# Moving the tasks of a software pipeline: attention and soft MoE on one core

## The chip, the cores and the metric

The kernel runs on one core of a Trainium2 chip. The metric is the device time of one execution in microseconds (us). A core has five engines with a queue each: TensorE (PE, matmuls, with its weight loads PEld), VectorE (DVE), ScalarE (ACT), GpSimd (POOL) and SyncE (SP), which here issues the DMAs. Each engine works through its own instructions in the order in which the program wrote them, and waits on semaphores for data and for free buffers.

## The reference

Eight batches of eight heads of attention with rotary positions, 576 positions of 64 elements each, all in float32. Its output, 4608 rows of 512, goes into a soft mixture of eight experts with four slots each.

```
q, k = rotate(q), rotate(k)
scores = (q @ k.T) / 8 - rowmax
x = (softmax(scores) @ v), heads side by side          # 4608 x 512
logits = x @ phi                                       # 4608 x 32
slot_input = softmax over the 4608 rows(logits).T @ x
slot_out[e] = relu(slot_input[e] @ w1[e]) @ w2[e]      # w1: 8 x 512 x 1024, w2: 8 x 1024 x 512
out = softmax over the 32 slots(logits) @ slot_out
```

## The kernel before

The 64 heads are worked on in 32 pairs; a pair fills the 128 partitions with two heads of 64. For pair p, called task(p), the steps are these.

`load0`, `load1` fetch the two halves of the tile `x_in` (q and k, each as the vector and its swapped copy, 576 KB a half; two buffers), and `load_v` fetches v, 576 KB. `spin0`, `spin1` multiply by cosine and sine on GpSimd, in four pieces each; `join`, the half addition, adds the two products on VectorE; `high0`, `high1` (ScalarE) and `low` (VectorE) split q and k into a high and a low float16 part (`hl`).

`m00` to `m31` and `m_rem` make rough scores from the high parts on TensorE, and VectorE reduces each to negated row maxima (L179, L187). `m_min` combines them, `m_turn` transposes them on TensorE, `m_half` (ScalarE) scales them to float16 (`mr`), and `m_rows` sends them by two small DMAs into the tile `peak` (L207, L208): these are the peak rows.

`t0` to `t8` make the transposed scores of 64 keys each, the first three products from `hl`, and the last product from `lift` and `peak`, which subtracts the maximum within the PSUM accumulation; ScalarE takes the exponential (L225). `av0` to `av8` multiply the weights by v (L240), `o_out` copies the result. `add1`, `add2` add weights of several blocks (L255, L258), `total` sums over the keys on TensorE (L268), `total_out` copies the sums, `send` spreads them over partitions by four small DMAs (`rc`, L279), `recip` inverts, `spread` writes them to DRAM (`r_row`, L292), `widen` reads them back as a broadcast to 64 partitions per head (`rb`, L299), and `norm` multiplies on GpSimd (L302). `logits`, `logits_sum`, `natural`, `natural_out` and, after every fourth pair, the statistics and slot work (`stats`, carried out piece by piece by `step0` to `step3`) follow. `weights` loads one 512 KB tile of expert weights per pair, `trickle0` to `trickle3` load more late in the run.

All tiles of scores, maxima, sums and transposes share one PSUM pool, `ps_s`, of three buffers (`bank2`); the weighted sums have one buffer of their own.

The order of the work is written out by hand. The dictionary `WHEN` gives every task a number; a beat handles one pair's share of all stages. The number modulo 4 is the task's place within the beat, its whole quotient by 4 the distance in pairs: a task with -12.8752 stands at 3.1248 of the beat and is done for the pair four ahead.

```
beat = sorted((when % 4, int(when // 4), name) for name, when in WHEN.items())
...
for p in range(NPAIR):
    for _, back, name in beat:
        do(name, p - back)
```

Since one loop emits all instructions, the sorted numbers set the order in each engine's queue, SyncE's DMAs among them. A prologue ahead of it does the first pairs' early steps, in the order of the unreduced numbers. After the loop the experts' two layers and the combination run with the loads of the remaining weights.

Of the kernel before, what the change touches and what calls it, by code (L numbers as in the profile page):

```python
# [44 lines left out]
RC = 12  # L45
PIECE = 4
WHEN = {
# [3 lines left out]
    "m_turn": -1.3908, "m_half": -1.1886, "m_rows": -0.6451, "weights": 0.144, "t0": 0.2257, "t1": 0.2781,  # L51
# [4 lines left out]
    "total_out": 5.5512, "send": 5.5526, "sums_turn": 6.0, "sums_wide": 6.3, "norm_wide": 6.4, "logits_late": 7.0,  # L56
    "recip": 7.022, "logits_sum_late": 7.05, "natural_late": 7.3, "natural_out_late": 7.35, "spread": 7.402,
    "widen": 7.6028, "norm": 9.5444, "logits": 10.5707, "logits_sum": 10.5777, "stats": 11.0576, "natural": 11.351,
    "natural_out": 11.3913,
}  # L60
QL, QH, KH, KL = range(4)
SUMS = ((0, 0, 0, True, False), (1, 0, 1, True, False), (2, 1, 0, True, False), (3, 1, 1, True, False),
# [873 lines left out]
```

## Time and profile before

| | before |
|---|---|
| time, median of 3 runs | 637.4 us (629.55 to 638.51) |
| the profiled execution | 634.23 us, span 632.4 us |
| TensorE busy | 547.5 us (87%) |
| VectorE busy | 447.0 us (71%) |
| ScalarE busy | 321.5 us (51%) |
| GpSimd busy | 283.5 us (45%) |
| SyncE's DMA queue | 110.15 MB, 52.7% of 16 engines' span |

Busy times come from one execution with a profiler; the span runs from its first instruction to its last. In a list of waits, "A <- B: total, times, longest" says how long engine A sat idle until B released it. In an answer by time, the columns are start, duration, engine, line, operation, output<-inputs, count, and in brackets the idle time before and what ended it; SPq is SyncE's issuing of a DMA, not the transfer. Rows that merge several instructions have the time from the first's start to the last's end.

### The profile page before, as it was taken

To read this page: it belongs to the slowest core of one execution; us is meant where nothing else is said; L and a number is where in the kernel's file an instruction comes from. 1 tells how busy PE (TensorE), PEld (TensorE's weight loads), DVE (VectorE), ACT (ScalarE), POOL (GpSimd) and SP (SyncE) were. 2 spreads that over 40 slices of the span, in tenths; PEclk is the share of its full clock that TensorE was granted. 3 is DMA by queue.
4 is the path that set the end of the run, shared out by engine and by line. 5 is a ranking of instruction groups with operands and counts; after the bars stand their busy time and mean duration, and the time that the engine had idled before them with its cause. 6 is when DMAs were issued, how large, how long until landed. Compare 5 with 4: busy or idle time off the path is not lost.

```text
span 632.4 us, 23700 instructions
## 1 busy us (share of the span) xinstructions
PE 547.5 (87%) x10320; PEld 368.5 (58%) x10320; DVE 447.0 (71%) x697; ACT 321.5 (51%) x647; POOL 283.5 (45%) x308
## 2 busy tenths in 40 slices
PE   3678979899988998898889998988899999799971
PEld 1356766666665666566666666666666666544550
DVE  6778757878877897688788988987889653222441
ACT  2145535566555555455555555655556554335341
POOL 2676654465456466544655655646556000100000
PEclk9679879999999999899999999999999999859995
DMA  7153434545554554455554545555542453549997
GB/s 263 46 188 115 142 120 168 168 168 169 169 167 167 168 169 168 167 168 163 174 168 166 170 165 170 169 167 170 167 135 98 128 194 126 177 142 345 348 373 258
DMA packets 71736, 111.66 MB, mean 177 GB/s; under 512 B 20176, under 2 KB 47568, under 8 KB 71632
## 3 DMA queue, kind: packets, MB, share of 16 engines
q1 hardware_dynamic: 71618, 110.15, 52.7%
q8 instruction: 81, 1.33, 0.9%
q14 instruction: 23, 0.19, 0.1%
q10 hardware_dynamic: 14, 0.00, 0.0%
HBM read 99.93 MB, written 9.58 MB: 173 GB/s over the span
## 4 chain that ended last, share of the span: by engine, by line
PE 54%; DMA 22%; DVE 11%; SPq 5%; ACT 3%; issue 2%; POOL 1%; ACTq 0%; POOLq 0%; DVEq 0%
PE s_ps L224 17%; DMA peak<-mr 14%; PE o_ps L240 11%; DVE nm L179 8%; PE s_ps L268 7%; PE s_ps L177 3%; PE s_ps L775 3%; DMA rb<-r_row 2%; SPq L279 2%; DMA r_row<-rr 2%; DMA x_in<-in_qk 2%; PE s_ps L351 1%; DMA w_exp<-in_w 1%; SPq L139 1%; ACT a_t L225 1%
## 5 line engine op out<-in xcount | busy, mean ns | idle before, releaser
L144 POOL TENSOR_TENSOR x_in<-x_in,cs_sb 128x288 f32<-128x288 f32 x248 | 231.6, 965 | 172.9 <-DMA x_in<-in_qk 163.1
L179 DVE TENSOR_REDUCE nm<-s_ps 128x2 f32<-128x576 f32 x256 | 186.2, 747 | 68.7 <-PE s_ps L177 68.0
L225 ACT ACTIVATE a_t<-s_ps 128x576 f32<-128x576 f32 x256 | 156.2, 648 | 90.7 <-PE s_ps L224 90.2
L240 PE MATMUL o_ps<-a_t,v_in 64*64 64x288 f32 x2048 | 168.6, 409 | 0.0
L224 PE MATMUL s_ps<-hl 64*64 64x288 f16 x3456 | 163.4, 289 | 5.3 <-DVE nm L179 2.6
L224 PEld LDWEIGHTS <-hl 64*64 64x64 f16 x3456 | 101.9, 107 | 45.0 <-issue 26.8
L224 PE MATMUL s_ps<-peak,lift 64*64 64x288 f16 x1152 | 98.9, 288 | 33.0 <-DMA peak<-mr 33.0
L177 PE MATMUL s_ps<-hl 64*64 64x288 f16 x1024 | 92.3, 295 | 11.5 <-DVE nm L179 7.6
L302 POOL TENSOR_TENSOR xt<-xt,rb 128x576 f32<-128x576 f32 x30 | 44.5, 1482 | 80.4 <-DMA rb<-r_row 48.8
L240 PEld LDWEIGHTS o_ps<-a_t,v_in 64*64 64x64 f32 x2048 | 75.2, 135 | 9.0 <-issue 0.2
L224 PEld LDWEIGHTS <-lift 64*64 64x64 f16 x1152 | 47.4, 108 | 40.5 <-issue 37.2
L273 ACT ACTIVATE s<-s_ps,bits 128x576 f32<-128x576 f32 x32 | 23.7, 740 | 85.2 <-PE s_ps L268 52.6
L177 PEld LDWEIGHTS <-hl 64*64 64x64 f16 x1024 | 47.9, 108 | 28.8 <-issue 21.1
L153 ACT CAST hl<-x_in 128x576 f16<-128x576 f32 (+1 forms) x66 | 40.6, 668 | 27.1 <-DVE x_in L148 25.3
L148 DVE TENSOR_TENSOR x_in<-x_in 128x1152 f32<-128x1152 f32 (+2 forms) x36 | 54.1, 1501 | 0.2
L255 DVE TENSOR_TENSOR c_t<-a_t 128x1152 f32<-128x1152 f32 x32 | 49.7, 1554 | 0.0
L157 DVE TENSOR_TENSOR hl<-x_in,hl 128x1152 f16<-128x1152 f32 x32 | 43.3, 1352 | 1.8 <-ACT hl L153 1.8
L268 PE MATMUL s_ps<-a_t,pick 128*32 128x288 f32 x384 | 36.7, 406 | 0.0
L343 ACT COPY xn<-s_ps 128x512 f32<-128x512 f32 x31 | 18.1, 585 | 19.3 <-PE s_ps L338 19.3
L248 ACT COPY xt<-o_ps 128x576 f32<-128x576 f32 x32 | 20.4, 638 | 12.1 <-PE s_ps L177 10.5
L240 PE MATMUL o_ps<-a_rem,v_in 64*64 64x288 f32 x256 | 25.8, 429 | 0.0
L187 DVE TENSOR_REDUCE nm<-s_ps 128x2 f32<-128x576 f32 x32 | 24.2, 758 | 0.8 <-PE s_ps L185 0.7
(182 smaller groups left out, 570.9 us busy)
## 6 DMA issues: line engine op xcount, KB each, us to landing
x_in<-in_qk SPq DMA_DIRECT2D x62, 576.0 KB
w_exp<-in_w SPq DMA_DIRECT2D x63, 512.0 KB
v_in<-in_v SPq DMA_DIRECT2D x32, 576.0 KB
rb<-r_row SPq DMA_DIRECT2D x60, 144.0 KB
out<-w_exp SPq DMA_DIRECT2D x16, 512.0 KB
rc<-s SPq DMA_DIRECT2D x120, 4.5 KB
x_in<-in_qk SPq DMA_DIRECT2D x4, 288.0 KB
out<-w_exp SPq DMA_DIRECT2D x4, 256.0 KB
```

What stands on the lines that cost most here:

```text
L144: eng.tensor_tensor(out=x[:, :, c], in0=x[:, :, c], in1=cs_sb[:, :, c], op=ALU.mult)
L148: nc.vector.tensor_tensor(out=x[:, t, 0, c], in0=x[:, t, 0, c], in1=x[:, t, 1, c], op=ALU.add)
L153: nc.scalar.copy(out=halves[p][:, 1 + t, c], in_=loaded[p][:, t, 0, c])
L157: nc.vector.tensor_tensor(out=hl[:, 0:4:3], in0=x[:, :, 0], in1=hl[:, 1:3], op=ALU.subtract)
L177: nc.tensor.matmul(s[rows[c], h, 0:HC], lhsT=hl[rows[h], QH, at:at + D], rhs=hl[rows[h], KH, half[n]], start=True, stop=True)
L179: nc.vector.tensor_reduce(out=nms[p][:, n, j:8:4], in_=s[:, :, 0:HC], axis=AX.X, op=ALU.max, negate=True)
L224: nc.tensor.matmul(s[rows[h ^ n], n, 0:HC], lhsT=lhs, rhs=rhs, start=(i == 0), stop=(i == 3))
L225: nc.scalar.activation(out=weights_of(p, b).rearrange("p (n x) -> p n x", n=2), in_=s[:, :, 0:HC], func=AF.Exp, scale=SCALE)
L240: nc.tensor.matmul(o[rows[h], n, 0:HC], lhsT=vt[r, b, n], rhs=a[r, half[n]], start=(b == 0), stop=(b == KB - 1))
L255: nc.vector.tensor_tensor(out=cts[p], in0=ats[p, 0], in1=ats[p, 1], op=ALU.add)
L268: nc.tensor.matmul(s[32 * i:32 * i + 32, n, 0:HC], lhsT=pick[:, n:n + NS], rhs=parts[cut][:, half[n]], start=first, stop=last, tile_positi ...
L302: eng.tensor_tensor(out=xts[p], in0=xts[p], in1=rbs.pop(p), op=ALU.mult)
```

## The change

Only the numbers in `WHEN` change. Which task does what, the buffers and the number of instructions are the same.

```diff
 WHEN = {
-    "load0": -16.0394, "load1": -12.8752, "spin0": -12.5438, "spin1": -11.4414, "join": -10.1083, "high0": -9.9771,
-    "high1": -9.8619, "low": -8.1718, "m01": -6.5475, "m00": -6.4604, "m10": -5.9309, "m11": -4.775, "m30": -3.8413,
-    "m20": -3.4941, "m21": -3.3162, "m31": -2.704, "m_rem": -2.4607, "m_min": -2.4496, "load_v": -2.2365,
-    "m_turn": -1.3908, "m_half": -1.1886, "m_rows": -0.6451, "weights": 0.144, "t0": 0.2257, "t1": 0.2781,
...
-    "t6": 3.0107, "av3": 3.0866, "av4": 3.222, "t7": 3.2246, "av5": 3.3, "t8": 3.4636, "trickle3": 3.55,
...
+    "load0": -16.2417, "load1": -12.7505, "spin0": -12.4293, "spin1": -12.3499, "join": -10.0149, "high0": -9.1292,
+    "high1": -9.0398, "low": -8.2534, "m01": -7.7418, "m11": -6.537, "m10": -5.8043, "m00": -5.1521, "m20": -3.9275,
+    "m21": -3.6837, "m30": -3.1916, "load_v": -2.9774, "m_rem": -2.8225, "m31": -2.6694, "m_min": -1.8172,
+    "m_turn": -1.7661, "m_half": -1.4738, "m_rows": -1.4517, "t0": -0.3716, "weights": 0.144, "t1": 0.1908,
...
+    "t6": 3.0107, "av4": 3.0368, "step2": 3.2977, "t7": 3.3041, "t8": 3.3085, "av5": 3.3336, "step3": 3.3449,
...
 }
```

Sorted by their places within a beat (the pair's distance from p in brackets), the tasks that put something on SyncE's queue and on the engines around the peak rows stand so:

```
SyncE before:   weights, trickle0, trickle1, send(-1), load_v(+1), trickle2, load1(+4), m_rows(+1),
                spread(-1), trickle3, widen(-1), load0(+5)
SyncE after:    weights, trickle0, load_v(+1), trickle1, send(-1), m_rows(+1), trickle2, load1(+4),
                spread(-1), widen(-1), trickle3, load0(+5)
TensorE before: av6(-1), m30(+1), t0, t1, av7(-1), m20(+1), av8(-1), m21(+1), t2, t3, m31(+1), av0, m01(+2),
                av1, m_rem(+1), m00(+2), total(-1), t4, t5, m10(+2), av2, logits(-2), m_turn(+1),
                t6, av3, av4, t7, m11(+2), av5, natural(-2), t8
TensorE after:  m20(+1), t1, av7(-1), m01(+2), av8(-1), m21(+1), t2, m30(+1), av0, m_rem(+1), t3, m31(+1), av1,
                m11(+2), total(-1), t4, t5, m10(+2), av2, av3, m_turn(+1), logits(-2), m00(+2),
                t6, av4, natural(-2), t7, t8, av5, av6, t0(+1)
VectorE before: m30, add2(-1), m20, m21, m31, m01, m_rem, m00, m_min(+1), join(+3), m10, logits_sum(-2), add1,
                recip(-1), m11, low(+3)
VectorE after:  m20, m01, m21, m30, m_rem, m31, m11, join(+3), m_min(+1), m10, logits_sum(-2), m00, add1,
                recip(-1), add2, low(+3)
GpSimd before:  spin1(+3), norm(-2), spin0(+4)
GpSimd after:   norm(-2), spin0(+4), spin1(+4)
```

An m unit stands in TensorE's list for its matmuls and in VectorE's for its reduction. The steps of the statistics are left out here: `step1` and `step2` stood together behind m10 before, and stand ahead of `total` and ahead of t7 after; `step0` follows av8 in both, `step3` follows t8 before and av5 after.

More of the change, by code (lines that the diff above doesn't have):

```diff
@@ L47 @@
 WHEN = {
[3 rows of a table removed]
-    "m_turn": -1.3908, "m_half": -1.1886, "m_rows": -0.6451, "weights": 0.144, "t0": 0.2257, "t1": 0.2781,
[4 rows of a table removed]
[L56 to L59, printed above, removed]
[3 rows of a table added]
+    "m_turn": -1.7661, "m_half": -1.4738, "m_rows": -1.4517, "t0": -0.3716, "weights": 0.144, "t1": 0.1908,
[4 rows of a table added]
+    "total_out": 5.55, "sums_turn": 6.0, "send": 6.1819, "sums_wide": 6.3, "norm_wide": 6.4, "logits_late": 7.0,
+    "logits_sum_late": 7.05, "recip": 7.2439, "natural_late": 7.3, "natural_out_late": 7.35, "spread": 7.3661,
+    "widen": 7.4052, "norm": 9.55, "logits": 10.7005, "logits_sum": 10.7559, "natural": 11.0423,
+    "natural_out": 11.2438, "stats": 11.3074,
 }
```

6 rows, old and new, of the table WHEN are left out of this document.

## Prediction

> **What bounds the kernel now.** I read the page's span and chain first, then the list of waits, then the DMA issues, the matmuls, VectorE and GpSimd of one repeated pair in the order of time.
>
> ```profile
> span 632.4 us, 23700 instructions
> ...
> PE s_ps L224 17%; DMA peak<-mr 14%; PE o_ps L240 11%; DVE nm L179 8%; PE s_ps L268 7%; PE s_ps L177 3%; PE s_ps L775 3%; DMA rb<-r_row 2%; SPq L279 2%; DMA r_row<-rr 2%; DMA x_in<-in_qk 2%; PE s_ps L351 1%; DMA w_exp<-in_w 1%; SPq L139 1%; ACT a_t L225 1%
> ```
> ```profile
> PE s_ps L224 <- DMA peak<-mr: 33.0, 22, 3.4
> ```
>
> The profiled execution took 634.23 us, of which 632.4 are the span. The chain that ended last is TensorE work, and the largest thing in it that is no work is the tiny DMA that puts the row maxima (the peak rows) into the tile `peak`: 14%. TensorE itself sat idle for it for 33.0 us in 22 waits.
>
> The steady part is one beat per pair of heads. I count beats by the four small DMAs of `send` (L279):
>
> ```profile
> 55.46 2.71 SPq L279 DMA_DIRECT2D rc<-s  x4
> ...
> 518.20 2.73 SPq L279 DMA_DIRECT2D rc<-s  x4
> ```
> ```profile
> 55.46:518.20 462.74, 421.30 (x8747) 294.69 (x8739) 369.38 (x557) 262.69 (x528) 244.06 (x250) 0.99 0.49 162
> ```
>
> From pair 0 to pair 29 that is 462.74 us for 29 beats: 15.96 us a beat. The second row is the table by stages (columns: length, busy time and count of PE, PEld, DVE, ACT, POOL, then granted clock, DMA share, GB/s). VectorE is busy 369.38 / 29 = 12.74 us of a beat, GpSimd 8.4; the granted clock is 0.99 and the DMA share 0.49, so neither is the limit as an average.
>
> One beat, by SyncE's queue:
>
> ```profile
> 299.59 2.74 SPq L279 DMA_DIRECT2D rc<-s  x4
> ...
> 315.27 2.73 SPq L279 DMA_DIRECT2D rc<-s  x4
> 318.10 0.39 SPq L163 DMA_DIRECT2D v_in<-in_v  x1
> 318.54 0.43 SPq L139 DMA_DIRECT2D x_in<-in_qk  x1
> 319.07 0.54 SPq L207 DMA_DIRECT2D peak<-mr  x1
> 319.65 0.54 SPq L208 DMA_DIRECT2D peak<-mr  x1
> 320.30 0.34 SPq L292 DMA_DIRECT2D r_row<-rr  x1
> 324.38 1.13 SPq L299 DMA_DIRECT2D rb<-r_row  x2
> ```
>
> `send` ends at 318.00. Before the peak rows (319.07) stand two large loads, v and the second half of x, 576 KB each. The same beat on TensorE, first the row of the chain for `total` (L268), then the matmuls in the order of time:
>
> ```profile
> 312.72 1.66 PE s_ps L268 x24
> ```
> ```profile
> 316.03 0.43 PE L351 MATMUL s_ps<-xt,phi_sb 128*32 128x128 f32 x8
> ...
> 316.50 0.28 PE L198 MATMUL s_ps<-id_sb,nm 128*9 128x128 f32 x1
> 316.70 0.56 PE L224 MATMUL s_ps<-hl 64*64 64x288 f16 x12
> ...
> 317.22 1.14 PE L240 MATMUL o_ps<-a_t,v_in 64*64 64x288 f32 x16
> 318.19 0.54 PE L224 MATMUL s_ps<-hl 64*64 64x288 f16 x12
> ...
> 318.80 0.66 PE L240 MATMUL o_ps<-a_t,v_in 64*64 64x288 f32 x8
> 319.39 0.66 PE L337 MATMUL s_ps<-id_sb,xt 128*128 128x128 f32 x4
> ...
> 320.08 0.56 PE L224 MATMUL s_ps<-hl 64*64 64x288 f16 x12
> ...
> 321.20 0.54 PE L224 MATMUL s_ps<-hl 64*64 64x288 f16 x12
> 323.60 0.54 PE L224 MATMUL s_ps<-peak,lift 64*64 64x288 f16 x4 [1.85 <-DMA peak<-mr]
> ```
>
> Durations overlap here, so I take the distance between starts as what a unit costs: scores t6 0.52, two weighted sums (av) 0.97, t7 with one m unit 0.61 (so t 0.50, m 0.11), `natural` 0.69, `logits` 0.47, `m_turn` 0.20. Let T be the start of `total`, 312.72. In t0 (321.20) the first twelve matmuls take three quarters of 0.50, so the peak rows are due at T+8.85; they come at T+10.88, 4.53 us after their first issue. **That is the wait, about 2 us in a beat, 33.0 in all.**
>
> **The change part by part.** No instruction is added or removed; tasks get other places. I sorted both tables by their fractional part to get each engine's order.
>
> *SyncE.* Before: send, v, x half 1, peak rows, r_row, broadcast rb, x half 0, weights. After: send, peak rows, x half 1, r_row, rb, x half 0, weights, v. The peak rows then issue when `send` ends, T+5.28, the second of them T+5.9, if `mr` is ready. From issue to landing without a large load ahead I have the row of `rc`: the last quarter of `send` begins at 317.32 and VectorE has its data at 319.55 (below), 2.2 us. So they land at T+8.1. The bounds: 2.2 us from the second issue, or, if the loads ahead were not the reason, 4.53 from the first (T+9.8). I take 2.2, the row of the same size class.
>
> *TensorE.* After `total` come t4, t5, m10, av2, av3, `m_turn`, `logits`, m00, t6, av4, `natural`, t7, t8, av5, av6, t0. Summed: 1.66 + 1.00 + 0.11 + 0.97 = T+3.74 for `m_turn` (before T+3.78), +0.20 +0.47 +0.11 +0.52 +0.49 +0.69 +1.00 +0.97 = T+8.19 for t0, so the peak rows are due at T+8.56. They land 0.4 earlier: the wait goes. The cover is thin: 0.4 us of lateness anywhere between `total` and the peak issue shows again as a wait on TensorE.
>
> *VectorE.* It runs in order and holds the half addition (`join`, L148), the evacuations and the additions:
>
> ```profile
> 311.25 1.42 DVE L179 TENSOR_REDUCE nm<-s_ps 128x2 f32<-128x576 f32 x2 [0.42 <-PE s_ps L177]
> ...
> 314.00 1.35 DVE L148 TENSOR_TENSOR x_in<-x_in 128x1152 f32<-128x1152 f32 x1
> ...
> 316.63 0.36 DVE L363 TENSOR_TENSOR l_sb<-s_ps,l_sb 128x192 f32<-128x192 f32 x1 [0.21 <-PE s_ps L354]
> 316.91 1.83 DVE L255 TENSOR_TENSOR c_t<-a_t 128x1152 f32<-128x1152 f32 x1
> 319.55 0.23 DVE L285 TENSOR_REDUCE rr<-rc 96x12 f32<-96x48 f32 x1 [0.81 <-DMA rc<-s]
> ...
> 321.06 1.35 DVE L157 TENSOR_TENSOR hl<-x_in,hl 128x1152 f16<-128x1152 f32 x1
> ...
> 323.00 0.75 DVE L258 TENSOR_TENSOR c_t<-c_t,a_t 128x576 f32<-128x576 f32 x1
> ```
>
> Two m evacuations come every 1.42 us. At T two of them are still queued in either order, so `join` starts near T+1.28 again (314.00). But `m_min`, which `m_turn` needs, now stands behind `join` instead of ahead: it is done at T+2.8 to T+3.3, for a `join` of 1.35 to 1.83 (the length to which the like addition L255 is drawn out), and due at T+3.74. Hidden, with 0.4 to 0.9 to spare.
>
> What is late next is VectorE itself. Its own work is 12.74 us a beat, and it must wait once: after m10 it stands at about T+3.7, and `logits` is done at T+4.41 plus the hand-over (0.2 in the row of L363), 0.9 us of idleness that no order of its own removes. That makes 13.6 us, the floor of the new beat. Today VectorE's larger idleness lies behind the peak wait. The floor assumes that nothing else collides; the first scores t0 now come ahead of m20 instead of behind m30, and seven m units in a row want VectorE between t0 and `total`, with only three score banks in PSUM.
>
> *Sum.* Two ways. Taking the wait alone: 33.0 / 29 = 1.14 a beat leaves 14.8. From the floor: half way between 13.6 and 15.96 is 14.8 too, half of the possible gain going to late beats (every fourth pair adds the statistics and slot work) and collisions. I take 14.8: 29 x 1.16 = 33.6 us less, 634.23 - 33.6 = **601 us**. The prologue issues t0 of pair 0 a little earlier, the tail from 540 us on is the same code: zero, with 5 us either way.
>
> *GpSimd and the shared data path.* Its order does not change (norm, spin0, spin1), but its inputs move:
>
> ```profile
> 312.14 1.41 POOL L302 TENSOR_TENSOR xt<-xt,rb 128x576 f32<-128x576 f32 x1 [1.34 <-DMA rb<-r_row]
> 314.62 4.78 POOL L144 TENSOR_TENSOR x_in<-x_in,cs_sb 128x288 f32<-128x288 f32 x4 [1.07 <-DMA x_in<-in_qk]
> 323.65 3.05 POOL L144 TENSOR_TENSOR x_in<-x_in,cs_sb 128x288 f32<-128x288 f32 x4 [4.25 <-DMA x_in<-in_qk]
> ```
>
> Four rotations take 3.05 us, or 4.78 when `join` and the c_t addition of VectorE run beside them. In the new order the norm (r_row issued T+7.7, landing behind x half 1 near T+11, rb 4 us later) runs near T+15 to T+16.4, just where the next `join` is due (T+14.8+1.28). The Trainium skill (SBUF — State Buffer, Who interferes with whom) says that a VectorE instruction with two SBUF inputs and a GpSimd instruction that reads SBUF exclude each other for the whole instruction; by that rule, which the stretched 4.78 agrees with, `join` could be held up to one norm, 1.41 us, and by it alone the beat would be up to 15.9, rival B's end.
>
> **The rivals.**
>
> *A: the early issue does not shorten the flight.* If 4.53 us stays, the rows land at T+9.8, and 1.25 of the 2.0 us remain: 0.75 x 22 = 17 us gained, **617**. Against it: the rows of v and x directly ahead, and 2.2 us for rc.
>
> *B: `join` becomes late.* x half 1 now issues behind the peak rows, T+6.5. Before, it took 318.54 to 323.65 = 5.1 us to arrive behind v; at 4 to 5 it is there at T+10.5 to T+11.5, rotated by T+13.6 to T+16.3, and `join` is due at T+16.1. If it or the norm holds `join` by a micro-second, `m_min`, `m_turn` and the peak rows slip with it, and the beat returns to 15.4 to 15.9: **618 to 634, middle 626**.
>
> *C: slower, by the broadcast.* x half 1 stands between the peak rows and r_row, so a large load is still ahead of r_row, rb and the norm, on which `logits` waits on TensorE. The chain of waits shows what that costs in a bad beat today:
>
> ```profile
> 207.81 4.46 DMA r_row<-rr
> ...
> 212.87 4.58 DMA rb<-r_row
> ...
> 217.60 2.54 POOL xt L302
> ```
>
> From 207.81 to 220.14 that is 12.3 us. With `recip` done at T+7.7, the norm ends at T+20.0, and `logits`, due at T+beat+3.94, makes the beat at least 16.1; with the 0.6 us by which step beats delay `recip`, 16.6: 29 x 0.65 = 19 more, **653**. It decides as soon as the three pieces exceed 10.9 us at a beat of 14.8. For it: the order in the queue. Against it: typical pieces are shorter (320.30 to 324.38 for r_row with twice the bytes ahead).
>
> *D: everything interleaves.* The beat comes to 13.6 to 14.2: 566 to 583, **575**.
>
> **How the numbers follow.** The forecast with its own range 588 to 616 gets 0.43, A 0.15, B 0.18, C 0.12, D 0.12. The range 582 to 636 takes in the forecast, A, B and the upper edge of D. 2%, about what a measurement can tell from no change, is 621.5 from the profiled time. Faster: the forecast, D and most of A, 0.67; within 2%: B and the rest, 0.21; slower: C, 0.12. The median of the runs shown, 637.4 (629.55 to 638.51), is 0.5% above the execution that I sum against.
>
> **What would show it.** Right: the wait of L224 for `peak` falls from 33.0 to under 8 us; the distance of `send` issues is near 14.8; peak rows issue directly behind `send` and land within 3 us; VectorE's busy share of the beat rises from 80% to 86%. Wrong: for A, 4 us between the peak issue and t0's last four matmuls; for B, VectorE idle ahead of L148, waiting for GpSimd; for C, TensorE idle ahead of L351, waiting for the norm; for D, no idleness of VectorE but ahead of L363. What would break the forecast most easily is the 0.4 us of slack between landing and t0.

## The result and the profile after

The changed kernel takes 595.5 us (median of 4 runs, 591.76 to 599.64) against 633.9 us (4 runs) of the kernel before: a ratio of 0.940, 95% interval 0.929 to 0.950. The profiled execution took 599.64 us, against 634.23 before. The forecast was 601, in a range of 582 to 636. Some executions show a lower granted clock and a longer time; the medians hold all runs, the ratios and their intervals leave those out, so a ratio need not be the quotient of the times beside it.

The page of the changed kernel, its span and its chain:

```profile
span 597.9 us, 23724 instructions
...
PE o_ps L240 14%; PE s_ps L224 14%; DMA rc<-s 7%; PE s_ps L268 6%; DVE nm L179 4%; PE s_ps L177 4%; DVE hl L157 3%; SPq L279 3%; PE s_ps L775 3%; DMA x_in<-in_qk 2%; DVE x_in L148 2%; DMA out<-w_exp 2%; PE s_ps L337 2%; DVE c_t L258 1%; DMA r_row<-rr 1%
```

The peak rows, 14% of the chain before, are no longer among the lines that the page lists for the chain. The waits, first of the changed kernel, then the two of before that the prediction did not show:

```profile
DVE nm L179 <- PE s_ps L177: 21.9, 28, 3.7
DVE l_sb L363 <- PE s_ps L354: 17.9, 22, 2.2
...
DVE l_sb L361 <- PE s_ps L354: 9.3, 8, 3.1
...
PE s_ps L224 <- DMA peak<-mr: 0.6, 3, 0.2
```
```profile
DVE nm L179 <- PE s_ps L177: 68.0, 84, 4.8
...
DVE l_sb L363 <- PE s_ps L354: 4.5, 12, 1.6
```

TensorE's wait for the peak rows went from 33.0 to 0.6 us. VectorE's wait for rough scores went from 68.0 to 21.9, and part of that idleness turned up ahead of `logits_sum` (L363, L361). The steady part, from the `send` of pair 0 to that of pair 29, in the table by stages:

```profile
57.25:486.95 429.70, 415.45 (x8763) 280.40 (x8755) 366.71 (x558) 264.64 (x528) 238.97 (x251) 1.00 0.54 173
```

429.70 / 29 = 14.82 us a beat, where the prediction had 14.8. The span divides so: ahead of the first `send` 57.25 (before 55.46, +1.8), the 29 beats 33.0 less, behind them 110.95 (before 114.20, -3.3): together 34.5 us less.

The same table tells where the 33.0 us of the beats come from. TensorE was idle for 41.4 of the 29 beats' 462.7 us before (462.74 - 421.30) and is idle for 14.3 of 429.7 now: 27.2 us less idleness, and 5.9 us less of its own work, though the matmuls are the same. Part of that last term can be seen in the granted clock. In the kernel before it falls to about half at three of the waits for the peak rows, those that end at 63.65, 82.54 and 258.55. Here is the second:

```profile
78.63 0.54 PE L224 MATMUL s_ps<-hl 64*64 64x288 f16 x12
82.54 0.63 PE L224 MATMUL s_ps<-peak,lift 64*64 64x288 f16 x4 [3.37 <-DMA peak<-mr]
82.73 1.15 PE L224 MATMUL s_ps<-hl 64*64 64x288 f16 x12
```

A group of twelve score matmuls takes 0.54 us ahead of that wait and 1.15 behind it; the mean granted clock is 0.57 from 64 to 68, 0.57 from 81 to 89 and 0.66 from 258 to 263, and these stretches lie in the three longest beats (17.24, 19.91 and 18.39 us). The changed kernel has one such stretch in its 29 beats, 267.9 to 272.0 with 0.58, behind a wait of 1.87 us at `m_turn`; e1 below has none. An estimate from these clocks and lengths: 6.9 us lost to them before, 1.7 after.

One beat of the changed kernel, SyncE, then TensorE's `total`, `m_turn` and t0, then VectorE and GpSimd of the next beat:

```profile
280.61 2.73 SPq L279 DMA_DIRECT2D rc<-s  x4
283.45 0.53 SPq L207 DMA_DIRECT2D peak<-mr  x1
284.03 0.53 SPq L208 DMA_DIRECT2D peak<-mr  x1
284.60 0.40 SPq L139 DMA_DIRECT2D x_in<-in_qk  x1
285.38 0.33 SPq L292 DMA_DIRECT2D r_row<-rr  x1
288.81 1.83 SPq L299 DMA_DIRECT2D rb<-r_row  x2
290.76 0.50 SPq L139 DMA_DIRECT2D x_in<-in_qk  x1
291.31 0.44 SPq L485 DMA_DIRECT2D w_exp<-in_w  x1
291.85 0.41 SPq L163 DMA_DIRECT2D v_in<-in_v  x1
294.35 3.82 SPq L279 DMA_DIRECT2D rc<-s  x4
...
298.86 0.53 SPq L208 DMA_DIRECT2D peak<-mr  x1
```
```profile
278.06 0.69 PE L268 MATMUL s_ps<-c_t,pick 128*32 128x288 f32 x8
...
281.85 0.28 PE L198 MATMUL s_ps<-id_sb,nm 128*9 128x128 f32 x1
...
286.42 0.54 PE L224 MATMUL s_ps<-hl 64*64 64x288 f16 x12
286.79 0.29 PE L224 MATMUL s_ps<-peak,lift 64*64 64x288 f16 x4
```
```profile
292.60 1.35 DVE L148 TENSOR_TENSOR x_in<-x_in 128x1152 f32<-128x1152 f32 x1
293.86 0.17 DVE L191 TENSOR_REDUCE nm<-nm 128x9 f32<-128x18 f32 x1
...
296.40 0.36 DVE L363 TENSOR_TENSOR l_sb<-s_ps,l_sb 128x192 f32<-128x192 f32 x1 [0.90 <-PE s_ps L354]
```
```profile
293.23 1.99 POOL L302 TENSOR_TENSOR xt<-xt,rb 128x576 f32<-128x576 f32 x1 [1.56 <-DMA rb<-r_row]
```

Here `total` starts at T = 278.06. The peak rows issue directly behind `send`, and t0's last four matmuls follow its first twelve without a gap.

### The profile page after: what moved, and what is told of

The parts are those of the page before. It is cut to its first block, busy times and chain, and to the rows that moved or that the text cites. A ratio compares the mean times of both kernels' runs of the same rounds, so it can differ in the third digit from the quotient of the medians.

```text
span 597.9 us, 23724 instructions
## 1 busy us (share of the span) xinstructions
PE 540.1 (90%) x10320; PEld 354.7 (59%) x10320; DVE 444.0 (74%) x697; ACT 323.5 (54%) x647; POOL 276.3 (46%) x308
## 4 chain that ended last, share of the span: by engine, by line
PE 56%; DVE 16%; DMA 15%; ACT 4%; SPq 4%; issue 3%; POOL 1%; DVEq 0%; ACTq 0%
PE o_ps L240 14%; PE s_ps L224 14%; DMA rc<-s 7%; PE s_ps L268 6%; DVE nm L179 4%; PE s_ps L177 4%; DVE hl L157 3%; SPq L279 3%; PE s_ps L775 3%; DMA x_in<-in_qk 2%; DVE x_in L148 2%; DMA out<-w_exp 2%; PE s_ps L337 2%; DVE c_t L258 1%; DMA r_row<-rr 1%
## 5 line engine op out<-in xcount | busy, mean ns | idle before, releaser
L144 POOL TENSOR_TENSOR x_in<-x_in,cs_sb 128x288 f32<-128x288 f32 x248 | 222.1, 928 | 148.5 <-DMA x_in<-in_qk 129.5
L179 DVE TENSOR_REDUCE nm<-s_ps 128x2 f32<-128x576 f32 x256 | 183.0, 750 | 22.8 <-PE s_ps L177 21.9
L225 ACT ACTIVATE a_t<-s_ps 128x576 f32<-128x576 f32 x256 | 160.3, 647 | 69.5 <-PE s_ps L224 64.2
L240 PE MATMUL o_ps<-a_t,v_in 64*64 64x288 f32 x2048 | 163.6, 408 | 1.1 <-ACT xt L248 0.3
L224 PE MATMUL s_ps<-hl 64*64 64x288 f16 x3456 | 159.6, 287 | 1.3 <-DVE nm L179 1.2
L224 PEld LDWEIGHTS <-hl 64*64 64x64 f16 x3456 | 100.1, 107 | 37.3 <-issue 25.8
L177 PE MATMUL s_ps<-hl 64*64 64x288 f16 x1024 | 83.8, 298 | 15.1 <-DVE nm L179 10.3
L224 PE MATMUL s_ps<-peak,lift 64*64 64x288 f16 x1152 | 90.5, 285 | 0.6 <-DMA peak<-mr 0.6
L177 PEld LDWEIGHTS <-hl 64*64 64x64 f16 x1024 | 44.0, 107 | 38.2 <-issue 21.7
L148 DVE TENSOR_TENSOR x_in<-x_in 128x1152 f32<-128x1152 f32 (+2 forms) x36 | 47.9, 1330 | 2.3 <-POOL x_in L144 2.0
L224 PEld LDWEIGHTS <-lift 64*64 64x64 f16 x1152 | 38.6, 108 | 3.0 <-issue 1.8
L248 ACT COPY xt<-o_ps 128x576 f32<-128x576 f32 x32 | 20.4, 638 | 16.0 <-PE o_ps L240 15.5
L187 DVE TENSOR_REDUCE nm<-s_ps 128x2 f32<-128x576 f32 x32 | 24.2, 755 | 2.1 <-PE s_ps L185 1.3
L258 DVE TENSOR_TENSOR c_t<-c_t,a_t 128x576 f32<-128x576 f32 x32 | 25.2, 788 | 0.1
```

The lines of the kernel that those rows point to most:

```text
L144: eng.tensor_tensor(out=x[:, :, c], in0=x[:, :, c], in1=cs_sb[:, :, c], op=ALU.mult)
L148: nc.vector.tensor_tensor(out=x[:, t, 0, c], in0=x[:, t, 0, c], in1=x[:, t, 1, c], op=ALU.add)
L177: nc.tensor.matmul(s[rows[c], h, 0:HC], lhsT=hl[rows[h], QH, at:at + D], rhs=hl[rows[h], KH, half[n]], start=True, stop=True)
L179: nc.vector.tensor_reduce(out=nms[p][:, n, j:8:4], in_=s[:, :, 0:HC], axis=AX.X, op=ALU.max, negate=True)
L224: nc.tensor.matmul(s[rows[h ^ n], n, 0:HC], lhsT=lhs, rhs=rhs, start=(i == 0), stop=(i == 3))
L225: nc.scalar.activation(out=weights_of(p, b).rearrange("p (n x) -> p n x", n=2), in_=s[:, :, 0:HC], func=AF.Exp, scale=SCALE)
```

## The experiments

The theory (Q): the gain is the queue, the large loads no longer directly ahead of the peak rows. The main rival (O): the gain is the new order of matmuls and reductions. Each ratio is against the kernel before on the same chip. The edits are to `WHEN` unless shown otherwise.

### The loads alone: e1_loads_only

The two entries alone, cut out of their lines:

```diff
 (on the kernel before)
-"load_v": -2.2365   "load1": -12.8752
+"load_v": -2.9774   "load1": -12.64
```

> The order of before, with only two loads moved on SyncE's queue: v to the place it has after the change, and the second half of x directly behind the peak rows. Theory Q (the gain is the queue: no large load ahead of the peak rows) expects the wait of L224 for peak to fall from 33.0 us to under 8, a beat near 14.9 and about 600 to 606 us. Rival O (the gain is the order of the matmuls and reductions, which needs t0, m_turn and the m units in their new places) expects at most half of the gain, 615 us or more, with VectorE idle for L177 staying near 68 us.

597.0 us (591.38 to 603.28), ratio 0.934 (0.927 to 0.942); a beat of 14.74 us.

```profile
DVE nm L179 <- PE s_ps L177: 30.4, 63, 3.1
DVE rr L285 <- DMA rc<-s: 15.5, 16, 2.2
PEld s_ps L351 <- POOL xt L302: 11.0, 8, 1.8
...
PE s_ps L351 <- POOL xt L302: 6.9, 8, 1.3
...
PE s_ps L224 <- DMA peak<-mr: 0.2, 1, 0.2
```

On SyncE's queue v now stands ahead of `send` and the second half of x behind the peak rows. Two numbers out of 71 give the whole gain: the peak wait is gone (0.2 us), and VectorE's idleness for L177 fell with it, 68.0 to 30.4, in the old order of reductions. Rival O falls.

### The order alone: e2_order_only

```diff
 (on the changed kernel)
-"load_v": -2.9774   "load1": -12.7505
+"load_v": -1.5      "load1": -13.46
```

> The changed kernel with v and the second half of x put back directly ahead of the peak rows, behind send; all else as after the change. Theory Q expects the peak rows about 1 us later on the queue and their flight near 4.5 us again, so they land near T+10.9 where they are due near T+8.6: the wait comes back to 30 us or more, and the time to 625 to 640 us. Rival O expects the new order to keep most of the gain: under 610 us.

654.0 us, ratio 1.034 (1.027 to 1.042): slower than before, and slower than theory Q had said.

```profile
300.44 0.69 PE L268 MATMUL s_ps<-c_t,pick 128*32 128x288 f32 x8
...
308.80 0.54 PE L224 MATMUL s_ps<-hl 64*64 64x288 f16 x12
311.37 0.48 PE L224 MATMUL s_ps<-peak,lift 64*64 64x288 f16 x4 [2.04 <-DMA peak<-mr]
```
```profile
DVE nm L179 <- PE s_ps L177: 75.5, 79, 3.0
...
PE s_ps L224 <- DMA peak<-mr: 48.0, 29, 3.2
```

The rows land at T+10.9, as in the kernel before, and the wait is back, 48.0 us in 29 waits where before had 33.0 in 22. The rest of the change, 56 other numbers, thus costs 3.4% when the rows are late, and e1 beside the changed kernel (0.934 and 0.940) shows no gain of it when they are early.

### One load moved: e3_load1_only

Before, with `load1` at -12.64 alone.

> The order of before with only the second half of x moved behind the peak rows; v stays directly ahead of them. If each 576 KB ahead delays the landing by its own transfer (about 1.7 us at the 340 GB/s of the busiest stretches) and 0.5 us of issuing, the rows land near T+8.7 and are due at T+8.85: theory Q expects most of the wait to go, 5 to 15 us of it left, and 605 to 612 us. If the number of loads ahead did not matter and any large load costs the whole flight of 4.5 us, 20 us of wait would stay: 620 us.

603.1 us, ratio 0.950 (0.944 to 0.957), and 3.6 us of peak wait in 5 beats. With one 576 KB load ahead the rows are almost in time, with two they are 2 us late: the delay grows with what stands directly ahead, as the expectation of this run reckoned. Whether it counts bytes or transfers this run does not tell apart, since both loads are of one size. Of the 1.6% to e1 only 3.4 us of wait are on the peak rows; TensorE's waits for the norm at L351 are larger too (weight loads 17.2 us against 11.0, matmuls 11.1 against 6.9; the two overlap).

### The loads on another queue: e9_other_queue

```diff
 (on the kernel before)
-        nc.sync.dma_start(out=loaded[p][:, t], in_=qk[p, t])
+        (nc.scalar if t and p > 3 else nc.sync).dma_start(out=loaded[p][:, t], in_=qk[p, t])
-        nc.sync.dma_start(out=vts[p], in_=v[p])
+        (nc.scalar if p else nc.sync).dma_start(out=vts[p], in_=v[p])
```

> The order of before, but v and the second half of x are issued from ScalarE's queue instead of SyncE's, at the same places of the program. They then start about when they start now, yet the peak rows issue right behind send (T+5.3 instead of T+6.35) and share no queue with them. If the cost of the loads ahead is the queue itself, the peak rows land 2 to 3 us after their first issue, the wait falls under 8 us and the time to 598 to 608 us. If the cost is the moving of 1152 KB on the same DMA engines, whatever the queue, only the earlier issue is gained: 10 us or more of wait stay, 612 us or more.

669.8 us, ratio 1.058 (1.045 to 1.072). Neither expectation foresaw this. The peak wait is gone (1.6 us), but another has taken its place:

```profile
DVE rr L285 <- DMA rc<-s: 93.4, 30, 5.3
```
```profile
318.21 0.33 ACTq L163 DMA_DIRECT2D v_in<-in_v  x1
...
320.13 0.33 ACTq L139 DMA_DIRECT2D x_in<-in_qk  x1
```
```profile
317.87 4.32 SPq L279 DMA_DIRECT2D rc<-s  x4
```
```profile
326.10 0.23 DVE L285 TENSOR_REDUCE rr<-rc 96x12 f32<-96x48 f32 x1 [4.75 <-DMA rc<-s]
```

v now starts while `send` is issuing, on ScalarE's queue, and the small `rc` transfers take from 317.87 to 326.10, 8.2 us, where before had 315.27 to 319.55, 4.3 us. VectorE stands at `recip` and everything behind it is late. So the delay is not SyncE's queue alone: here a small transfer was late with large ones issued beside it on another queue. How fast the peak rows themselves land this run does not show, since TensorE now waits for VectorE ahead of them (67.3 us at L177), and in the whole run its mean granted clock is lower too (0.97 from 60 to 520, where before has 0.99 from 55.46 to 518.20). The Trainium skill (DMA: Bandwidth & Descriptors, Issuing engines are not separate DMA queues) says that DMAs from the different issuing engines run on the same 16 DMA engines and interleave; the trace agrees, with 8.2 against 4.3 us.

### The places of single tasks

`t0` back behind m20 (`"t0": 0.1` in the changed kernel):

> The changed kernel with t0 put behind the first m unit of the next beat (m20) instead of ahead of it. Theory Q expects no loss, the same within 1% (591 to 603 us), as the peak rows only get 0.1 us more slack. Rival O expects the place of t0 to matter, since it gives TensorE work while VectorE finishes the low parts: 5 to 15 us slower than the changed kernel.

599.7 us, ratio 0.946 (0.940 to 0.952), within the scatter of the changed kernel. The place of t0 is worth nothing that shows.

`m_min` ahead of the half addition (`"m_min": -2.02` in the changed kernel):

> The changed kernel with m_min put back ahead of join on VectorE. The prediction held the moved half addition hidden, with 0.4 to 0.9 us to spare ahead of m_turn: then nothing changes, 591 to 603 us. If m_min is late behind join in many beats (rival), m_turn comes up to 1 us earlier and the time falls by 5 to 15 us.

593.4 us, ratio 0.938 (0.930 to 0.946). No difference in the time: the moved half addition is hidden, as predicted. In the changed kernel TensorE does wait at `m_turn` for `m_min` five times, 4.0 us in all, and here that wait is gone, but 4.0 us do not stand out of the scatter.

`load1` behind the broadcast too (`"load1": -12.4` in the changed kernel):

> The changed kernel with the second half of x moved behind the broadcast (rb) as well, some 5 us later on SyncE's queue. r_row and rb then fly with nothing large ahead: the norm comes 1 to 2 us earlier. But x arrives near T+16 and is rotated by T+19, while join is due near T+16: join should wait about 3 us a beat, VectorE idle for L144 by some 60 to 90 us, and the time 640 to 680 us. If join had 3 us or more to spare, the time would stay at 590 to 600 us.

680.4 us, ratio 1.075 (1.066 to 1.084).

```profile
325.32 2.54 DVE L148 TENSOR_TENSOR x_in<-x_in 128x1152 f32<-128x1152 f32 x1 [3.81 <-POOL x_in L144]
```
```profile
PE s_ps L198 <- DVE nm L191: 69.9, 27, 6.0
DVE x_in L148 <- POOL x_in L144: 66.0, 24, 6.2
```

`join` waits for the rotation, `m_min` stands behind it, and TensorE waits at `m_turn`: VectorE is idle for 66.0 us and TensorE for 69.9, as reckoned. The time rose by more, 85 us over the changed kernel: behind many of these waits the granted clock falls (behind the 3.59 us that end at 328.08 it is about 0.50 until 333), and its mean from 60 to 520 is 0.93, which is 32 us of TensorE's full speed by estimate (460 x 0.07). Rival B's mechanism is real; the changed kernel's place for `load1` is just early enough.

`logits` ahead of av3 and `m_turn` (`"logits": 10.21` in the changed kernel):

> The changed kernel with logits moved ahead of av3 and m_turn on TensorE, 0.7 us earlier; VectorE's idleness ahead of L363 and L361 is 27 us in the changed kernel. If VectorE's order sets the beat, as the prediction's floor says, 10 to 20 us are gained: 577 to 588 us. If TensorE sets it, nothing changes, 591 to 600 us; if the norm is not done by then, TensorE waits for it and the time rises by up to 10 us.

598.8 us, ratio 0.947 (0.936 to 0.957): no gain.

```profile
DVE nm L179 <- PE s_ps L177: 37.3, 55, 2.9
...
DVE l_sb L363 <- PE s_ps L354: 9.6, 16, 1.7
...
DVE l_sb L361 <- PE s_ps L354: 3.6, 6, 2.4
```

VectorE's wait for `logits` fell from 27.2 to 13.2 us, and its wait for rough scores rose from 21.9 to 37.3. Its idleness moved; it was not what set the beat. The third thing that was expected came in part: TensorE's wait for the norm at L351 grew from 2.4 to 4.3 us on the matmuls and from 3.0 to 12.6 on the weight loads.

`recip`, `spread`, `widen` behind `low` (7.748, 7.7482, 7.7484 in the changed kernel):

> The changed kernel with recip, spread and widen put behind low. VectorE no longer waits for rc (9.8 us) ahead of add2 and low, so the next m units start earlier: 3 to 8 us gained if VectorE sets the beat. Against it, r_row issues about 2 us later, and the norm, which had 0.5 to 1.5 us to spare ahead of logits, comes late: TensorE should wait for it by 15 to 40 us at L351, and the time rise to 605 to 630 us. I expect the second.

600.6 us, ratio 0.946 (0.939 to 0.952). TensorE waits 8.6 and 6.1 us at L351, less than I had said, and nothing is won.

`recip` behind m11 (`"recip": 7.3` on top of e1):

> The order of before with the two loads moved, and recip put behind m11 on VectorE (spread stays behind it). VectorE waited 15.5 us for rc in the run with the loads moved alone; m11's reduction fills 0.67 us of that in each beat. If VectorE's order is on the chain there, 5 to 10 us are gained, 587 to 592 us; if the chain runs over TensorE in those beats, the time stays at 592 to 600 us, and the norm, 0.7 us later, can cost up to 5 us on L351.

599.1 us, ratio 0.942 (0.935 to 0.948): VectorE's wait for `rc` fell from 15.5 to 2.7 us and the time did not; its wait for rough scores rose from 30.4 to 38.5 us.

### Why the new order is the worse one under late rows

Two runs on top of e2: t0 behind m20, and then behind m20, m01 and m21 (`"t0": 0.1`; then also `"m01": -7.93, "m21": -3.928`).

> The changed order with v and the second half of x back ahead of the peak rows, and t0 put behind m20 as well. If the new order is slower under the late peak rows because the m units of the next beat stand behind the waiting t0, so that VectorE has nothing to reduce during the wait, then this gives VectorE one unit and TensorE the same wait: VectorE's idleness for L177 falls by 10 us or more from 75.5, and the time from 654 to 636 to 646 us. If the loss has another cause, such as m_min behind join, the time stays at 648 to 660 us.

648.8 us against 635.7 of before. The four runs took 641.04, 644.07, 653.60 and 661.39 us, too far apart to tell this from e2; the lower two lie in the 636 to 646 that was expected of a gain. But the sign that was named with it did not come: VectorE's idleness for L177 is 74.1 us, where e2 had 75.5.

> As the run with the changed order, the late peak rows and m20 ahead of t0, but with m01 and m21 ahead of t0 too: three of the seven m units that stood behind t0. If the new order loses against the order of before because more reductions stand behind the waiting t0, VectorE now does three of them (2 us) during the wait, its idleness for L177 falls by 30 us or more, and the time comes to 615 to 640 us. If the loss has another cause, it stays at 641 to 661 us.

653.2 us, ratio 1.026 (1.016 to 1.037).

```profile
328.84 0.56 PE L224 MATMUL s_ps<-hl 64*64 64x288 f16 x12 [2.15 <-DVE nm L179]
```

The peak wait is nearly gone by name (2.4 us), but TensorE now waits ahead of t0 for VectorE instead (45.3 us in 30 waits), and VectorE's idleness for L177 is 77.5 us. So nothing supports the explanation that the loss comes from the reductions behind t0; with the new wait in its place, the run does not clear it wholly either.

The traces of before and e2 show where most of the loss stands. The profiled execution of e2 is 12.1 us longer than that of before, and its peak wait 15.0 us longer. Before, every fourth pair's slot work (L398, L401) stood between `total` and t0, and in those beats t0 came so late that the late rows cost nothing; after the change it stands ahead of `total`. First before, in the beat with T at 136.81, then e2, in the beat with T at 135.92:

```profile
140.46 1.06 PE L401 MATMUL s_ps<-xn,dn 128*32 128x512 f32 x8
...
147.83 0.29 PE L224 MATMUL s_ps<-peak,lift 64*64 64x288 f16 x4
```
```profile
135.04 1.06 PE L401 MATMUL s_ps<-xn,dn 128*32 128x512 f32 x8
...
146.90 0.48 PE L224 MATMUL s_ps<-peak,lift 64*64 64x288 f16 x4 [1.70 <-DMA peak<-mr]
```

There are six such beats up to pair 29. Before, they hold 0.2 us of peak wait together; in e2 they hold 1.70, 2.49, 1.70, 1.62, 1.31 and 1.62, 10.4 in all. That is 10.2 of the 15.0 us. No run puts the slot work back alone, so this is read from two traces and not tested, and the rest stays open.

## Why the prediction was right, point by point

**The bound.** The peak rows behind two large loads were what held the beat: e1 moves those two loads and nothing else, and gains 6.6%. Right.

**The early issue and the flight.** Predicted: issue at T+5.28 and T+5.9, landing by T+8.1. With T at 278.06 they issue at T+5.39 and T+5.97. The landing itself shows in no row, since nobody waits any more; t0 takes them at T+8.73. In the next beat `send` is stretched to 3.82 us, the second issue comes at 298.86, and t0 took the rows without a wait at 300.53:

```profile
300.16 0.54 PE L224 MATMUL s_ps<-hl 64*64 64x288 f16 x12
300.53 0.29 PE L224 MATMUL s_ps<-peak,lift 64*64 64x288 f16 x4
```

That is at most 1.67 us of flight where I had taken 2.2 from `rc`. By 2.2 this beat would have shown 0.5 us of waiting; the term was a little too large, in the safe direction. Rival A (4.5 us whatever stands ahead) is refuted.

**TensorE's walk.** `m_turn` predicted at T+3.74, found at 281.85, T+3.79; t0 predicted at T+8.19, found at T+8.36. Right.

**The half addition ahead of `m_min`.** Predicted hidden: `m_min` done by 294.03, `m_turn` in that beat due at about 295.6, and e5 shows no difference. Right in most beats; in five TensorE waited for it, 4.0 us in all.

**The collision on the shared data path.** It is there in the beat above: the norm begins at 293.23 inside `join` (292.60 to 293.95), and takes 1.99 us where 1.41 is usual. GpSimd paid, not VectorE, whose `join` stayed at 1.35; VectorE's wait for GpSimd at `join` is 2.0 us in the whole run. The rule that the two exclude each other, which the prediction takes from the Trainium skill (SBUF — State Buffer, Who interferes with whom), nearly agrees: held until 293.95 and then 1.41 us long, the norm would end at 295.36, and its row ends at 295.22. Rival B's price did not come in this beat, where the norm started second. The 15.9 that the prediction gives for the beat by that rule does not follow from its terms; 14.8 + 1.41 is 16.2.

**The floor.** Predicted 13.6 us, from 12.74 of VectorE's work plus 0.9 of waiting for `logits`, and "half way" from there to 14.8. The quiet beats came to 13.74 to 14.1 (280.61 to 294.35 is 13.74), and the wait ahead of L363 in the beat shown to exactly 0.90. But the step was wrong in its reason. In that beat VectorE is busy for 11.57 us of the 13.74, and TensorE for 13.62. Over the 29 beats TensorE is busy for 415.45 / 29 = 14.33 us of 14.82, so its work leaves the mean beat little room below 14.82, and hardly any for rival D's 13.6 to 14.2; the prediction's own table had it at 421.30 / 29 = 14.53 before, and the floor did not use it. This also fits e7 and e11, which took 14 and 13 us from two waits of VectorE and gained nothing: VectorE's wait for rough scores rose instead. (The ends of matmuls are modelled in the profile, so the busy time is not exact.) That half way gave the right number is luck.

The other way, 33.0 / 29 off the beat, is the one that the runs support, though not one for one: 32.4 us of peak wait went, and 33.0 us of beats, but of these only 27.2 are idleness of TensorE, and 5.9 are shorter work, the clock behind the long waits included, of which the prediction knew nothing.

**The sums.** Three are off by little, and nothing hangs on them: rival B's beat of 15.9 gives 632, not 634; rival C decides when its three pieces exceed 11.0 us, not 10.9 (14.8 + 3.94 - 7.7); and 15.9 above. Of the signs named for being right, the last came too: VectorE's busy share of the beat rose to 85% (366.71 of 429.70), where 86% was forecast.

**What I left unsaid.** The prediction read the change as one whole. It did not say that the reordering of matmuls and reductions shows no gain, and under late rows costs 3.4%.

**The slower rival.** Rival C, the broadcast behind `load1`, did not decide: TensorE's waits for the norm at L351 are 2.4 us on the matmuls in the changed kernel, as before, and 3.0 on the weight loads. r_row to rb took 285.38 to 288.81, 3.4 us, less than the 4.1 of before with two loads ahead.

No version here beats the changed kernel clear of the scatter; e1 and e5 equal it.

## What to carry to other kernels

A tiny transfer on which a busy engine waits can be late for the large loads issued just ahead of it: look for the small DMA in the chain, read which large loads were issued in the 2 us ahead of it, and move them away, well ahead of it or behind it, to a place where their own consumer can still take them; e6 shows what a place too late costs. Moving them to another engine's queue was no shelter here: another small transfer was late instead. When a change moves many things, run its smallest part alone: here two numbers gave the whole gain, and the rest showed its cost only when that part was taken out. And before an engine's idle time is taken away, look which engine is busy for nearly the whole beat: here TensorE was, and VectorE's idle time was worth nothing.

## What the runs showed of the hardware

SyncE's issuing itself takes longer with large loads issued just ahead or beside it: four `rc` DMAs take 2.73 us to issue at 280.61, 3.82 us at 294.35, behind x, weights and v issued from 290.76 to 292.26, and 4.32 us in e9 with v starting beside them. A small transfer with no large load issued in the 6 us ahead of it landed within 1.67 us of its issue (298.86 to 300.53), while 1152 KB ahead of it made that 3.95 (319.65 to 323.60). And a wait of TensorE can cost more than its own length: behind the 3.37 us at 82.54 the granted clock stayed low until about 88, and twelve matmuls took 1.15 us in place of 0.54. Not every wait did this; the one of 2.10 us that ended at 178.91 shows no fall of the clock. So a forecast that takes off the wait alone can be too small.
